# Two transformer layers on one core: ten weight loads issued with the MLP's groups instead of in a row

## The chip, the core and the metric

The kernel runs on one core of one Trainium2 chip. A core has five engines with queues of their own: TensorE (PE) multiplies matrices, VectorE (DVE) and ScalarE (ACT) work element by element, GpSimd (POOL) does small side work, and SyncE (SP) issues DMA transfers. ACT and POOL can issue transfers too. Each queue is worked off in order, and engines wait for each other by semaphores. The time is the device time of one execution in microseconds (us), the median of several runs.

## The reference

The input is 2048 rows of 512 numbers in bf16. The same two blocks, attention and MLP, are applied twice with the same weights. Each is added to its input, and each starts with a layer norm without gain or offset.

```python
def _A_ref(x, wqkv, wo):            # H = 32 heads of Dh = 16
    qkv = transpose((x @ wqkv).reshape(B, S, 3, H, Dh), 2, 0, 3, 1, 4)
    q, k, v = qkv[0], qkv[1], qkv[2]
    scores = jnp.einsum("bhqd,bhkd->bhqk", q, k) * (Dh ** -0.5)
    p = softmax(scores, axis=-1)
    o = jnp.einsum("bhqk,bhkd->bhqd", p, v)
    return transpose(o, 0, 2, 1, 3).reshape(B, S, D) @ wo

def _B_ref(x, w1, w2):              # w1 512 x 1792, w2 1792 x 512
    h = jnp.maximum(jnp.einsum("bsd,df->bsf", x, w1), 0)
    return jnp.einsum("bsf,fd->bsd", h, w2)

x = A_x
x = x + _A_ref(layernorm(x), A_wqkv, A_wo)
x = x + _B_ref(layernorm(x), B_w1, B_w2)
x = x + _A_ref(layernorm(x), A_wqkv, A_wo)
x = x + _B_ref(layernorm(x), B_w1, B_w2)
```

## The kernel before

**Chunks and segments.** The rows are cut into chunks `(l, j)`: four of 512 rows in the first layer (l = 0), and in the second (l = 1) two of 512 and four of 256, numbered j = 0 to 5. The attention of a chunk runs in segments, one for each half of a group of heads (T = 0 to 3, e = 0 or 1), so eight a chunk. In a segment the scores of blocks of 128 keys are made in `ps_s` (L1356), turned into exponentials `e` on ScalarE (L1365) or, for some blocks, by a chain of five steps on VectorE (`lin` L1051, `step` L1092, `cube` L1103 and L1107), and multiplied with the values into `ps_o` (L944).

**The end of a segment** (`finish_segment`, L828). VectorE copies `ps_o` into `u` (L858), among it the sums of the softmax. These few rows are brought into a compact shape by a small DMA on SyncE, `c<-u` (L863, 4 KB for 256 rows). VectorE takes the reciprocal (L885), and a second small DMA on SyncE brings it back, `u<-c` (L886). Then the reciprocals are spread over the lanes: for most segments by a DMA on GpSimd, `r<-u` (L888), for the last of a chunk by a shuffle on VectorE (L898). A multiplication (L874) gives `ot`. After the last segment of a chunk, the rest of that chunk's work is appended to a list.

**The rest of a chunk** (`rest_of_chunk`, L754): the product with `wo`, the norm, the first MLP product in groups (`h_group`, L687), the second (`z_group`), and in the first layer the next layer's keys and values. TensorE does these in pieces, between the scores of the chunks that follow.

**The weights of the first MLP product.** `w1` doesn't stay in the on-chip memory. Four buffers `w1buf` of 128 columns each are used in turn. A group of a 256-row chunk takes two of them, so there are seven groups; as soon as its last matmul has been written out, `after()` (L707) has SyncE load the two buffers again (`load_w1`, L677, its transfer at L681), which waits for TensorE to be done with them. The groups write through `ps_f` (L445), and VectorE applies the maximum with zero (`ht`, L701).

**The last 256 rows.** Their MLP is done at the end, in a part of its own, and finds all 14 blocks of `w1` in place: four in `w1buf`, ten in the buffers `kt01` and `kt2`, which held keys in the first layer and partial sums after that. The list `w1_last` names the 14 places (read at L1465). Where the ten are loaded is written in `rest_of_chunk`, when it is called for chunk (1, 3):

```python
if (l, j) == (1, LAST - 2):
    for ft in range(NF):
        home = (...)
        w1_last.append(home)
        if ft >= NW1:
            nc.sync.dma_start(out=home, in_=B_w1[:, ft * P : (ft + 1) * P]...)   # L766
```

**What sets the order.** The program keeps modelled clocks for TensorE, VectorE and ScalarE, and writes out instructions in the order these suggest. It allows a fixed time for each transfer: `C_LAG` 3600 ns from the copy to the reciprocal, `U_LAG` 3000 ns from the reciprocal to the shuffle, and 4000 ns for a load of `w1`. The load of the ten blocks takes no part in these clocks. The order on every engine is therefore fixed when the program is built, and SyncE's queue holds its transfers in the order in which they were written out.

Of the kernel before, what the change touches and what calls it, by code (L numbers as in the profile page):

```python
# [25 lines left out]
def kernel(  # L26
# [10 lines left out]
    nc = tc.nc  # L37
    P = 128
# [208 lines left out]
    def mark(key, engine="dve", lag=0.0):  # L247
        made[key] = (engine, (now_pe if engine == "pe" else now_dve)[0] + lag)

    def at(keys, engine):  # L250

        t = 0.0
        for k in keys:
            if k not in made:
                return None
            e, when = made[k]
            if e != engine:
                when += PE_TO_DVE if engine == "dve" else DVE_TO_PE
            elif e == "dve":
                when += DVE_TO_DVE  # L260
            t = max(t, when)
        return t
# [42 lines left out]
    def start_group(g):  # L305
        (urgent if g in urgent else work).remove(g)
        ready = max(at(g["deps"], "pe"), bank_free[0] + DVE_TO_PE)
        cur.extend((c, fn, ready if n == 0 else 0.0) for n, (c, fn) in enumerate(g["pieces"]))
# [28 lines left out]
    def do_task(t):  # L337
        dve_q.remove(t)
        dve_run(t["cost"], at(t["deps"], "dve"))
        t["fn"]()  # L340
        for k in t["makes"]:
            if k not in made:
                mark(k)
# [40 lines left out]
    def finish_group():  # L384
        while cur:
            do_piece()
        while evac:
            do_evac()
# [24 lines left out]
    def run_all():  # L413
        while True:
            finish_group()
            g = next(
                (g for q in (urgent, work) for g in q if at(g["deps"], "pe") is not None), None
            )
            if g is not None:
                start_group(g)  # L420
            elif dve_q:
                do_task(next(t for t in dve_q if at(t["deps"], "dve") is not None))
            else:
                break
        assert not (urgent or work)

    def mm_group(mms, fin, makes, deps, per=1, cost=EVAC, after=None, wide_by=QS, sums=1):


        hold = {}  # L430
        pieces = []
        n = len(mms)
        for a in range(0, n, per):

            def piece(a=a):
                if a == 0:
                    hold["b"] = bank()[:, 0 : sums * wide_by]
                b = hold["b"]
                for i in range(a, min(a + per, n)):
                    lhsT, rhs = mms[i]  # L440
                    k = n // sums
                    out = b[:, i // k * wide_by : (i // k + 1) * wide_by]
                    for g in range(4):
                        cols = slice(32 * g, 32 * g + 32)
                        nc.tensor.matmul(  # L445
                            out[cols], lhsT[:, cols], rhs, start=i % k == 0,
                            stop=i % k == k - 1, tile_position=(0, 32 * g),
                            skip_group_check=True,
                        )
                if a + per >= n:  # L450
                    put_evac(cost, lambda: fin(b))
                    if after:
                        after()

            pieces.append((min(per, n - a) * wide_by / QS, piece))
        return group(pieces, makes, deps)
# [8 lines left out]
    def columns(l, j):  # L465

        tt, n = chunks[l, j]
        return tt // TPC, tt % TPC * P, n * P
# [117 lines left out]
    def each(n, *key):  # L586
        return [key + (i,) for i in range(n)]
# [8 lines left out]
    def k_group(l, T, j):  # L596
        return mm_group(
            k_mms(T, j), lambda b: k_fin(l, T, j, b), [("k", l, T, j)],
            each(TPC, "xnT", ("ln1", l, j)),
        )  # L600
# [76 lines left out]
    def load_w1(n):  # L677

        if n < len(chunks) * NF - NF + NW1:
            ft = n % NF  # L680
            nc.sync.dma_start(  # L681
                out=w1buf[n % NW1][:],
                in_=B_w1[:, ft * P : (ft + 1) * P].rearrange("(c p) f -> p c f", p=P),
            )
            mark(("w1", n), "pe", 4000.0)

    def h_group(l, j, ft, war):  # L687
        n = (l * NQS + j) * NF + ft
        xj, a, w = columns(l, j)

        number = QS // w
        fts = range(ft, ft + number)
        made_here = [("h", l, j, f) for f in fts]

        def fin(b):
            out = htp[ft // 2][:, ft % 2 : ft % 2 + number, a : a + w]
            sums = b.rearrange("p (f q) -> p f q", f=number)
            if ending[0]:
                nc.scalar.activation(out=out, in_=sums, func=ACTF.Relu)
            else:  # L700
                nc.vector.tensor_scalar(  # L701
                    out=out, in0=sums, scalar1=0.0, scalar2=None, op0=ALU.max
                )
            for key in made_here:
                mark(key)

        def after():  # L707
            for f in range(number):
                load_w1(n + f + NW1)

        return mm_group(
            [
                (w1buf[(n + f) % NW1][:, c, :], xnT[xj][:, c, a : a + w])
                for f in range(number) for c in range(NDC)
            ],
            fin, made_here,
            each(w // P, "xnT", ("ln2", l, j)) + war + [("w1", n + f) for f in range(number)],
            after=after, wide_by=w, sums=number,
        )

# [19 lines left out]
    def before(l, j):  # L740

        if (l, j) == (0, 0):
            return None
        if not j:
            return 0, NQS - 1
        rows = chunks[l, j][0] % TPC
        return max(
            (l, b) for b in range(j)
            if chunks[l, b][1] == TPC or chunks[l, b][0] % TPC == rows
        )  # L750
# [3 lines left out]
    def rest_of_chunk(l, j):  # L754

        if (l, j) == (1, LAST - 2):
            for ft in range(NF):
                home = (
                    w1buf[((l * NQS + LAST) * NF + ft) % NW1] if ft < NW1
                    else (kt01 + kt2)[(ft - NW1) // 2][:, ft % 2, :].rearrange(  # L760
                        "p (c f) -> p c f", c=NDC
                    )
                )
                w1_last.append(home)
                if ft >= NW1:
                    nc.sync.dma_start(  # L766
                        out=home,
                        in_=B_w1[:, ft * P : (ft + 1) * P].rearrange("(c p) f -> p c f", p=P),
                    )
        b = before(l, j)  # L770
        xj, a, w = columns(l, j)
        n = w // P
        war_h = each(chunks[b][1], "z", *b) if b else []
        work[0:0] = [o_group(l, j, i) for i in range(n)] + ln_groups(
            ("ln2", l, j), xnT[xj], a, n, []
        )
        gs = [h_group(l, j, ft, war_h) for ft in range(0, NF, QS // w)]
        gs += [z_group(l, j, i) for i in range((l, j) == (1, LAST - 1), n)]
        if l == 0:
            gs += ln_groups(("ln1", 1, j), xnT[j], 0, TPC, [])  # L780
            gs.append(k_group(1, 0, j))
            gs += [v_group(1, kb) for kb in range(j * TPC, (j + 1) * TPC)]
            gs += [k_group(1, T, j) for T in range(1, 4)]
        return gs
# [344 lines left out]
    for e in range(2):  # L1129
        nc.vector.tensor_reduce(  # L1130
            out=mask[e],
            in_=ident[:].rearrange("p (g e d) -> p e g d", g=4, e=2)[:, e],
# [3 lines left out]
            out=qmask[:, e : e + 1], in0=mask[e], scalar1=SCALE * LOG2E * UNIT, scalar2=None,  # L1136
# [90 lines left out]
    while units:  # L1227
# [135 lines left out]
        while len(pend) == NE:  # L1363
            force_v()
        ex = nc.scalar.activation(  # L1365
            out=eb[:, 0 : place[m]], in_=b[:, 0 : place[m]], func=ACTF.Exp,
# [27 lines left out]
        run_dve(0.0, musts)  # L1394
    ending[0] = True
    run_all()
    ending[0], wide[0] = False, True
    users.clear()
    l, j = 1, LAST
# [11 lines left out]
    def at_bank(b):  # L1411
        n, w = b
        return ps_s[n][:, w, :] if n < 2 else (ps_f, ps_o)[n - 2][:]
# [46 lines left out]
    for ft in range(NF + 1):  # L1460
        if ft < NF:
# [6 lines left out]
            if ft % 2:  # L1468
                out = nc.scalar.activation(out=ht[ft][:, at_column : at_column + width], in_=at_bank(b)[:, 0:width], func=ACTF.Relu)
            else:  # L1470
                out = nc.vector.tensor_scalar(
                    out=ht[ft][:, at_column : at_column + width], in0=at_bank(b)[:, 0:width],
                    scalar1=0.0, scalar2=None, op0=ALU.max,
                )
# [7 lines left out]
    for i in rows:  # L1482
# [3 lines left out]
            out=out_flat[(tt + i) * P : (tt + i + 1) * P, :], in_=x_t[tt + i][:]  # L1486
# [31 lines left out]
```

The softmax here doesn't subtract the row's maximum and nothing guards it: scores larger than these inputs give would overflow.

## Time and profile before

| | |
|---|---|
| median of 4 runs | 1597.34 us (1596.12 to 1597.8) |
| profiled execution, its own time | 1597.56 us |
| its span, first to last instruction | 1595.7 us |
| ScalarE busy | 1554.3 us, 97% |
| VectorE busy | 1490.3 us, 93% |
| TensorE busy (matmuls) | 1441.6 us, 90% |
| mean granted TensorE clock | 0.993 |
| transfers at L681 (`w1`) | 130 of 128 KB |
| transfers at L766 (the ten blocks) | 10 of 128 KB, issued from 1373.5 to 1381.2 us |

Times in the views are us from the start of the span. In a list of waits, a row names the waiting engine, its line, what it waited for, the sum, the number of times and the longest. In a timeline, a row is start, duration, engine, line, operation, what is written from what, and how many instructions were merged; in brackets stands the idle time before it and what ended it. In a table of stretches, a row has its limits, its length, then for each engine the busy time and number of instructions (PE, weight loads, DVE, ACT, POOL), the granted TensorE clock, the share of the DMA engines and GB/s. SPq is SyncE's queue, in which a transfer's duration is that of its issue, not of the transfer.

### The profile page before, as it was taken

How to read it: one execution, taken by the hardware profiler on the slowest of the kernel's cores; microseconds unless marked ns; L12 is line 12 of the kernel's file. 1: busy time of each engine (PE TensorE's matmuls, PEld its weight loads, DVE VectorE, ACT ScalarE, POOL GpSimd, SP SyncE). 2: the span in 40 equal slices, each digit the busy share in tenths (PEclk: the TensorE clock that was granted, in tenths of full speed). 3: DMA queues.
4: the chain of work that ended last, by engine and by line, in shares of the span. 5: the costliest groups of instructions: out<-in, count | busy, mean ns of one | idle time of the engine just before them, and what ended most of it. 6: DMA issues, size and time to landing. Idle time of an engine off the chain costs nothing.

```text
span 1595.7 us, 45167 instructions
## 1 busy us (share of the span) xinstructions
PE 1441.6 (90%) x19793; PEld 538.0 (34%) x19793; DVE 1490.3 (93%) x2899; ACT 1554.3 (97%) x1383; POOL 98.3 (6%) x240
## 2 busy tenths in 40 slices
PE   8888888999999999899888999888999999899897
PEld 3322222322333222233222223222334444445444
DVE  6669999999999999999899999899999999899994
ACT  7999999999999999999999999999999999999994
POOL 2000001001010010100000000001000110010100
PEclk9999999999999999999999999999999999999999
DMA  5001100210012100120000100000211111413020
GB/s 166 2 1 23 20 11 11 46 29 11 7 22 44 20 15 5 30 46 10 14 2 11 31 8 1 2 4 8 55 24 20 33 36 26 93 20 65 14 61 16
DMA packets 115830, 42.42 MB, mean 27 GB/s; under 512 B 104785, under 2 KB 112721, under 8 KB 115633
## 3 DMA queue, kind: packets, MB, share of 16 engines
q1 hardware_dynamic: 101696, 26.21, 7.3%
q0 software_dynamic: 12592, 12.02, 4.2%
q8 instruction: 154, 2.52, 0.7%
q10 hardware_dynamic: 1344, 1.31, 0.2%
q14 instruction: 44, 0.35, 0.1%
HBM read 24.38 MB, written 2.10 MB: 17 GB/s over the span
## 4 chain that ended last, share of the span: by engine, by line
ACT 70%; PE 15%; DVE 11%; issue 2%; SPq 1%; DMA 0%; POOL 0%; ACTq 0%; DVEq 0%
ACT e L1365 70%; PE ps_s L1356 5%; PE ps_f L445 4%; PE ps_o L944 4%; DVE lin L1051 3%; DVE cube L1103 1%; DVE step L1092 1%; DVE cube L1107 1%; PE ps_s L1417 1%; DVE q L643 1%; DVE ht L701 1%; SPq L766 0%; DVE u L858 0%; DVE stats L479 0%; DVE x L727 0%
## 5 line engine op out<-in xcount | busy, mean ns | idle before, releaser
L1365 ACT ACTIVATE e<-ps_s 128x1536 bf16<-128x1536 f32 (+1 forms) x1366 | 1545.6, 1365 | 10.7 <-PE ps_s L1356 9.5
L1356 PE MATMUL ps_s<-q,ktp 32*128 32x512 bf16 (+1 forms) x6121 | 607.5, 342 | 104.7 <-ACT e L1365 94.8
L944 PE MATMUL ps_o<-e,vaug 128*32 128x512 bf16 (+1 forms) x4256 | 497.5, 346 | 12.0 <-DVE u L858 4.9
L1051 DVE TENSOR_SCALAR lin<-ps_s 128x512 int16<-128x512 f32 x684 | 465.4, 685 | 26.8 <-PE ps_s L1356 20.0
L1356 PEld LDWEIGHTS <-ktp 32*128 32x128 bf16 x6121 | 195.5, 92 | 553.1 <-issue 418.9
L944 PEld LDWEIGHTS <-vaug 128*32 128x32 bf16 x6036 | 171.9, 94 | 300.1 <-issue 283.5
L1092 DVE TENSOR_SCALAR step<-lin 128x1024 int16<-128x1024 int16 x684 | 268.9, 419 | 0.6
L1103 DVE TENSOR_TENSOR cube<-step 128x1024 f16<-128x1024 bf16 x342 | 231.8, 681 | 0.6
L1107 DVE TENSOR_TENSOR cube<-cube,lin 128x1024 bf16<-128x1024 f16 x342 | 232.2, 680 | 0.0
L944 PE MATMUL ps_o<-step,vaug 128*32 128x512 bf16 (+1 forms) x864 | 156.2, 340 | 2.7 <-DVE step L1092 2.7
L445 PE MATMUL ps_f<-xnT,w 128*32 128x512 bf16 (+1 forms) x2016 | 150.3, 346 | 6.2 <-DVE ht L701 2.8
L944 PE MATMUL ps_o<-cube,vthird 128*32 128x512 bf16 (+1 forms) x812 | 148.8, 338 | 0.5 <-DVE cube L1107 0.5
L445 PE MATMUL ps_f<-w,ht 128*32 128x512 bf16 x1624 | 146.8, 381 | 1.1 <-DVE q L643 0.8
L944 PE MATMUL ps_o<-lin,vaug 128*32 128x512 bf16 (+1 forms) x864 | 122.4, 340 | 4.8 <-DVE u L858 1.8
L888 POOL DMA_DIRECT2D r<-u x59 | 43.5, 737 | 1179.4 <-DVE lin L1051 426.5
L445 PE MATMUL ps_f<-xnT,wqkv 128*32 128x512 bf16 (+1 forms) x1312 | 107.2, 362 | 5.6 <-DVE ktp L593 0.9
L445 PE MATMUL ps_f<-wo,ot 128*32 128x512 bf16 x960 | 86.3, 381 | 1.1 <-DVE ktp L593 0.8
L701 DVE TENSOR_SCALAR ht<-ps_f 128x512 bf16<-128x512 f32 x105 | 72.0, 685 | 2.5 <-PE ps_f L445 1.2
L445 PEld LDWEIGHTS <-w 128*32 128x32 bf16 x2016 | 59.5, 96 | 37.4 <-issue 21.7
L643 DVE TENSOR_TENSOR q<-ps_f,masks 128x1024 bf16<-128x1024 f32 (+1 forms) x51 | 53.6, 1051 | 12.4 <-PE ps_f L445 7.7
L944 PEld LDWEIGHTS <-vthird 128*32 128x32 bf16 x812 | 44.6, 95 | 30.8 <-issue 27.1
L445 PEld LDWEIGHTS <-ht 128*32 128x32 bf16 x1624 | 45.3, 96 | 28.3 <-issue 12.2
(103 smaller groups left out, 637.6 us busy)
## 6 DMA issues: line engine op xcount, KB each, us to landing
w<-in_B_w_dram SPq DMA_DIRECT2D x130, 128.0 KB
r<-u POOLq DMA_DIRECT2D x32, 256.0 KB, 7.4
r<-u POOLq DMA_DIRECT2D x27, 128.0 KB, 4.9
out_dram<-x SPq DMA_DIRECT2D x16, 128.0 KB
x<-in_A_x_dram SPq DMA_DIRECT2D x14, 128.0 KB
w<-in_B_w_dram SPq DMA_DIRECT2D x1, 1792.0 KB
ktp<-in_B_w_dram SPq DMA_DIRECT2D x10, 128.0 KB
wqkv<-in_A_wqkv_dram ACTq DMA_DIRECT2D x2, 512.0 KB
```

What stands on the lines that cost most here:

```text
L445: nc.tensor.matmul(out[cols], lhsT[:, cols], rhs, start=i % k == 0, stop=i % k == k - 1, tile_position=(0, 32 * g), skip_group_check=True,)
L643: return nc.vector.tensor_mul(out=qbuf[n % 2][:, :, 0:w], in0=b.rearrange("p (e q) -> p e q", e=1).to_broadcast((P, 2, w)), in1=qmask.rear ...
L701: nc.vector.tensor_scalar(out=out, in0=sums, scalar1=0.0, scalar2=None, op0=ALU.max)
L888: nc.gpsimd.dma_start(out=r[:, 0:width], in_=bass.AP(tensor=sums.tensor, offset=sums.offset, ap=[list(sums.ap[0]), [0, 32], [1, width]],),)
L944: nc.tensor.matmul(ps_o[32 * g : 32 * g + 32, 0 : sg["w"]], values[:, 4 * sg["T"] + g, 2 * e : 2 * e + 32], rhs, start=g not in sg["begun" ...
L1051: first = nc.vector.tensor_scalar(out=lin[which][:, half * QS : (half + 1) * QS], in0=src, scalar1=EXP_BIAS, scalar2=0.0, op0=ALU.add, op1 ...
L1092: nc.vector.tensor_scalar(out=stair, in0=line, scalar1=keep, scalar2=put, op0=ALU.bitwise_and, op1=ALU.bitwise_or,)
L1103: (609, lambda: nc.vector.tensor_mul(out=power, in0=mantissa, in1=mantissa)),
L1107: (609, lambda: nc.vector.tensor_mul(out=power.bitcast(BF16), in0=power, in1=line.bitcast(BF16))),
L1356: nc.tensor.matmul(b[:, a : a + sg["w"]], kt[32 * g : 32 * g + 32, kc : kc + P], qbuf[sg["n"] % 2][32 * g : 32 * g + 32, sg["e"], 0 : sg[" ...
L1365: ex = nc.scalar.activation(out=eb[:, 0 : place[m]], in_=b[:, 0 : place[m]], func=ACTF.Exp, scale=1.0 / (LOG2E * UNIT),)
L1417: uses(nc.tensor.matmul(out, lhsT, rhs, start=first, stop=last), b, needs=needs)
```

## The change

The ten transfers are no longer issued in `rest_of_chunk`. It puts their places and block numbers into a list `w1_to_load` instead. Each time that `after()` of a group of the first MLP product is run, it issues the loads of that group's own buffers as before, and then takes one entry from the list, if there is one, and issues its load. At the end of the attention, an assertion says that the list is empty. The transfers themselves, their number and their places are the same.

```diff
+    w1_to_load = deque()
+
     def h_group(l, j, ft, war):
...
         def after():
             for f in range(number):
                 load_w1(n + f + NW1)
+            if w1_to_load:
+                home, of = w1_to_load.popleft()
+                nc.sync.dma_start(
+                    out=home,
+                    in_=B_w1[:, of * P : (of + 1) * P].rearrange("(c p) f -> p c f", p=P),
+                )
...
                 w1_last.append(home)
                 if ft >= NW1:
-                    nc.sync.dma_start(
-                        out=home,
-                        in_=B_w1[:, ft * P : (ft + 1) * P].rearrange("(c p) f -> p c f", p=P),
-                    )
+                    w1_to_load.append((home, ft))
...
     run_all()
+    assert not w1_to_load
```

## The prediction

> **What bounds the kernel.** The page comes first: ScalarE is busy for 97% of the span, nearly all of it the exponentials at L1365, and the busy slices show it full in the middle of the run. Whatever shortens the run must take out a gap between two exponentials. So the next view is the list of waits, cut to the stretch in which the ten loads are issued (1360 to 1470 us):
>
> ```profile
> ACT e L1365 <- PE ps_s L1356: 3.4, 2, 2.8
> DVE c L885 <- DMA c<-u: 3.3, 1, 3.3
> PE ps_o L944 <- DVE step L1092: 2.7, 1, 2.7
> ```
>
> Three engines stop once each for about 3 us, in a stretch where the exponentials otherwise lose nothing. The timelines of SyncE's queue, VectorE and ScalarE give the order:
>
> ```profile
> 1372.93 0.54 SPq L886 DMA_DIRECT2D u<-c  x1
> 1373.52 8.20 SPq L766 DMA_DIRECT2D ktp<-in_B_w_dram  x10
> 1381.81 0.56 SPq L863 DMA_DIRECT2D c<-u  x1
> 1382.48 2.29 SPq L681 DMA_DIRECT2D w<-in_B_w_dram  x4
> 1384.95 0.55 SPq L886 DMA_DIRECT2D u<-c  x1
> 1386.40 6.14 SPq L681 DMA_DIRECT2D w<-in_B_w_dram  x4
> ...
> 1376.40 0.41 DVE L858 COPY u<-ps_o 128x256 f32<-128x256 f32 x1
> ...
> 1383.79 0.20 DVE L885 RECIPROCAL c<-c 128x8 f32<-128x8 f32 x1 [3.31 <-DMA c<-u]
> ...
> 1387.34 0.44 DVE L898 STREAM_SHUFFLE r<-u 128x256 f32<-128x256 f32 x1
> ...
> 1386.85 1.45 ACT L1365 ACTIVATE e<-ps_s 128x1536 bf16<-128x1536 f32 x1 [2.82 <-PE ps_s L1356]
> 1388.87 3.52 ACT L1365 ACTIVATE e<-ps_s 128x1024 bf16<-128x1024 f32 x3 [0.57 <-PE ps_s L1356]
> ```
>
> The ten loads hold the queue for 8.2 us. Right behind them stands the 4 KB transfer c<-u (L863), which carries the softmax sums of the segment that has just ended. Its data are there at 1376.8 (the copy at 1376.40), but it starts at 1381.81, and VectorE, which works in order, stands at the reciprocal until 1383.79. TensorE then lacks step (L1092), and ScalarE lacks scores. The chain of waits runs through this place too: it names L766 ten times, then "DMA c<-u" for 1.95 us, then the reciprocal. One more view, the stretches of 3.41 us around it, with one from elsewhere that ends in the same way:
>
> ```profile
> 1380.11:1383.53 3.42, 2.70 (x71) 1.64 (x64) 0.37 (x1) 3.42 (x4) 0.00 (x0) 1.00 0.64 139
> 1383.53:1386.94 3.41, 1.40 (x39) 0.98 (x42) 3.15 (x8) 0.59 (x2) 0.00 (x0) 1.00 0.71 157
> 1386.94:1390.35 3.41, 3.41 (x60) 2.10 (x52) 3.01 (x8) 2.84 (x3) 0.00 (x0) 0.50 0.37 82
> 383.42:386.83 3.41, 2.16 (x22) 0.70 (x21) 3.41 (x8) 3.41 (x5) 2.88 (x6) 1.00 0.01 2
> ```
>
> The number after POOL's is the granted TensorE clock: after the stretch in which TensorE was busy for only 1.40 us it falls to 0.50 for 3.41 us.
>
> **What the gap costs.** Exponentials overlap a little, so I take start to start: undisturbed, 0.90 us for 1024 columns and 1.33 us for 1536 (medians of the trace). Around the gap: 1382.89 to 1386.85 is 3.97 us for a 1024, a loss of 3.06; 1386.85 to 1388.87 is 2.02 for a 1536, a loss of 0.69; 1389.79 to 1390.94 is 1.15 for a 1024, a loss of 0.24. Sum 3.99 us: the first term is the wait, the other two lie in the half-clock stretch. From there to 1560 us ScalarE stays full, so everything later moves up by what is won here.
>
> **The change, part by part.**
>
> *Removed: ten loads in a row.* c<-u then starts when the copy is done. Elsewhere the copy takes about 0.44 us from its start to the start of c<-u (copy at 1393.12, c<-u at 1393.56), so it starts at 1376.85 and with 1.95 us lands at 1378.8. VectorE reaches the reciprocal at 1380.40 (the op ahead starts at 1379.80 and holds the engine for 0.60). Slack 1.6 us: this wait goes.
>
> *Added: one load behind each group's own two w1 loads.* Which groups? The list is filled where the ten were issued. In the queue before, eight w1 loads stand behind the ten and ahead of 1393 us: four groups of two, still of the third chunk of layer two. So four loads go with them, and six with the fourth chunk's groups (1436 to 1459 us), not with the fourth and fifth. Call the four groups A to D. One load takes SyncE about 0.51 us to issue (five of the ten; 1.2 to 1.6 us when the queue is backed up).
>
> *What they push back.* The new order is c<-u, A's two loads and one more, B's two and one more, u<-c, then C and D. A w1 load waits for TensorE to be done with the buffer it overwrites: B's second load can go at 1381.2 us, when B's matmuls end. It takes 0.4, the added load 0.5, the queue's own waits 0.1: u<-c starts at 1382.27 and, at 2.0 us like c<-u, lands at 1384.27. Who waits for it is the shuffle at L898. Before, it came 3.55 us after the reciprocal; now 1380.40 + 3.55 = 1383.95, and some later, as two operations ahead of it need TensorE's results first (ht needs B's, about 0.15 us; lin needs the scores issued at 1382.19, about 0.15). So it is due near 1384.25, just as its data land. Bounds: nothing, to 0.75 us with u<-c 0.5 us late and the shuffle 0.25 early; I take nothing to 0.1, because u<-c took 2.0 us at 1384.95 with four w1 loads just ahead.
>
> *C and D.* Their reloads come behind 0.5 us more each, D's end near 1393.1 on the old clock against the next c<-u at 1393.56. No cost; without that half microsecond, c<-u would slip into a lag of some 4 us.
>
> *Fourth chunk.* The tightest place is c<-u at 1440.08, directly behind four w1 loads: two added loads put it to about 1440.6. Its reciprocal ran at 1445.13, 2.8 us after the landing of about 1442.3: covered. The last loads are issued by 1457 us; their first use is in the last rows' MLP, after 1577 us. Cost nothing. Bytes, matmuls, activations and the order on the other engines stay.
>
> *The clock.* [...] By the rows, half clock follows stretches that are merely thin: 1.40 us busy here, 2.16 at 383 us, while 2.70 left the clock alone. I take the rows: with the gap filled TensorE is busy for about 2.9 to 3.4 us of each stretch, and the drop goes.
>
> [...]
>
> *Sum.* 3.99, less about 0.15: TensorE resumes at 1382.63 instead of 1385.54, so the first scores are ready at about 1383.94, while ScalarE is free at 1383.80. 3.84, less up to 0.1 for the shuffle: 3.75 us. The profiled execution took 1597.56 us (span 1595.7), 0.2 us above the median, so 1593.8 there and **1593.6** against the median of 1597.34, 0.23% faster. A measurement of this kernel can tell about 0.2%, 3.2 us, from no change; the forecast is only just past it.
>
> **The rivals.**
>
> *The wait moves to u<-c.* u<-c now stands behind six weight loads, which an r<-u transfer (128 KB, 4.9 us median) shares the engines with until about 1380.5. If it lands 0.8 to 1.5 us late, the shuffle holds VectorE, which had nearly no slack in the old gap (3.31 us of wait became 3.06 of loss): gain 2.3 to 3.0, 1594.3 to 1595.1. For it: the planner allows 3 us from reciprocal to shuffle, and 2.0 of these are the transfer. Against: the 2.0 us at 1384.95 under a similar queue.
>
> [...]
>
> *The change does nothing it should:* something else stops VectorE at the same place, as the w1 reloads of A, which also came late before. They are issued at 1377.8 and 1378.5 now, and group C needs them at 1382.6; little room for this. About 1597.
>
> *Slower: TensorE waits for w1 in the fourth chunk.* The r<-u at 1435.6 makes w1 loads slow: the first was issued at 1436.02, landed about 1440.9, and is used at 1441.45, with 0.6 us to spare. Added loads share these engines. If each of the six takes the 1.6 us of the longest issue, pushed on from group to group, TensorE loses 6 x 1.6 - 0.6 = 9.0 us, net 5.2: 1602.5. It decides from about 1.2 us a load on. Against it: the added load stands behind its own group's reloads, and later groups have 2 us and more.
>
> **How the numbers follow.** Forecast 0.77, the wait at u<-c 0.11, the clock 0.04, nothing 0.03, slower 0.05. The forecast's own range is 1592.8 to 1594.4 (the bounds above and the spread of the medians, 1596.12 to 1597.8). The range reaches over the first two rivals and leaves out the last two: 1592.6 to 1595.8. Faster by over 0.2% means under 1594.15: most of the forecast, 0.69, and 0.01 of the rest; the u<-c and clock cases, the forecast's slow end and "nothing" are within 0.2%: 0.25; slower 0.05.
>
> **What would show it.** c<-u issued within 0.5 us of its copy near 1376.9; no DMA wait at L885; exponentials without a gap at 1383 to 1391; clock 1.00 there; four added loads ahead of 1393 us and six at 1433 to 1455. Wrong it would be if a wait stands at L898, at the matmuls that read w1, or if a half-clock stretch appears somewhere new.

## The result and the profile after

The changed kernel takes 1593.75 us (median of 35 runs, 1590.57 to 1599.33) against 1597.67 (56 runs) of the kernel before, so these medians differ by 3.92 us. The ratio on record is 0.9973, 95% interval 0.9966 to 0.9979, which would be 4.3 us less with an interval of 3.4 to 5.4. The forecast was 3.75 us less. Single executions spread over 9 to 11 us, more than the change is worth, so below one figure is used that is read inside a profile: **the interval** from the start of the `c<-u` of the segment before the chunk's last one to the first addition of the product with `wo` (`x<-x,ps_f`, L667). It holds the place of the change and leaves out what happens elsewhere. In the kernel before it runs from 1365.83 to 1397.46 us, 31.63; in the changed one from 1364.75 to 1392.64, 27.89. The difference is 3.74 us.

The changed kernel's timelines of SyncE's queue, VectorE and ScalarE at the same place (the added loads are now at L714, and later lines have moved by 2 to 8):

```profile
1371.85 0.54 SPq L891 DMA_DIRECT2D u<-c  x1
1375.77 0.56 SPq L868 DMA_DIRECT2D c<-u  x1
1376.44 1.74 SPq L681 DMA_DIRECT2D w<-in_B_w_dram  x2
1378.23 0.50 SPq L714 DMA_DIRECT2D ktp<-in_B_w_dram  x1
1379.70 1.05 SPq L681 DMA_DIRECT2D w<-in_B_w_dram  x2
1380.80 0.50 SPq L714 DMA_DIRECT2D ktp<-in_B_w_dram  x1
1381.46 0.54 SPq L891 DMA_DIRECT2D u<-c  x1
...
1375.33 0.41 DVE L863 COPY u<-ps_o 128x256 f32<-128x256 f32 x1
...
1379.33 0.19 DVE L890 RECIPROCAL c<-c 128x8 f32<-128x8 f32 x1
...
1383.65 0.43 DVE L903 STREAM_SHUFFLE r<-u 128x256 f32<-128x256 f32 x1
...
1373.68 26.52 ACT L1370 ACTIVATE e<-ps_s 128x1536 bf16<-128x1536 f32 x23
```

`c<-u` starts 0.44 us after the start of its copy, the reciprocal has no wait in its row, and 23 exponentials run without a gap. The list of waits of this kernel (1360 to 1470 us) has no wait at the reciprocal left, but a small new one:

```profile
PE ps_s L1361 <- ACT e L1370: 4.2, 13, 0.5
...
DVE r L903 <- DMA u<-c: 0.4, 1, 0.4
```

TensorE still waits for ScalarE, but no exponential waits for TensorE any more. In the table of stretches the half-clock stretch is gone:

```profile
1380.00:1383.41 3.41, 3.41 (x93) 2.21 (x90) 3.12 (x7) 3.41 (x4) 0.00 (x0) 1.00 0.65 141
1383.41:1386.82 3.41, 2.98 (x77) 1.82 (x74) 3.17 (x8) 3.41 (x4) 0.00 (x0) 1.00 0.52 117
```

Between the two profiled executions the time fell by 3.12 us (1597.56 to 1594.44), less than the 3.74. The changed kernel's profile is already 1.08 us ahead at 1365 us, far from the change, and it loses 1.68 us at the very end (29.42 us from the start of the last exponential to the end of the span, instead of 27.74). That part is taken up last.

### The profile page after: what moved, and what is told of

It reads as the page before. It is cut to its first block, busy times and chain, and to the rows that moved or that the text cites. A ratio compares the mean times of both kernels' runs of the same rounds, so it can differ in the third digit from the quotient of the medians.

```text
span 1592.5 us, 45173 instructions
## 1 busy us (share of the span) xinstructions
PE 1438.9 (90%) x19793; PEld 537.9 (34%) x19793; DVE 1490.2 (94%) x2899; ACT 1553.4 (98%) x1383; POOL 98.0 (6%) x240
## 4 chain that ended last, share of the span: by engine, by line
ACT 72%; PE 14%; DVE 11%; issue 2%; DMA 1%; POOL 0%; ACTq 0%; DVEq 0%
ACT e L1370 72%; PE ps_s L1361 5%; PE ps_f L445 4%; PE ps_o L949 4%; DVE lin L1056 3%; DVE cube L1108 1%; DVE step L1097 1%; DVE cube L1112 1%; PE ps_s L1423 1%; DMA wqkv<-in_A_wqkv_dram 1%; DVE ht L703 1%; DVE q L643 0%; DVE u L863 0%; DVE x L735 0%; DVE ktp L593 0%
## 5 line engine op out<-in xcount | busy, mean ns | idle before, releaser
L949 PEld LDWEIGHTS <-vthird 128*32 128x32 bf16 x812 | 44.3, 95 | 30.7 <-issue 27.1
```

The costliest lines, as they stand in the source:

```text
L949: nc.tensor.matmul(ps_o[32 * g : 32 * g + 32, 0 : sg["w"]], values[:, 4 * sg["T"] + g, 2 * e : 2 * e + 32], rhs, start=g not in sg["begun" ...
```

## The experiments

The theory, from the prediction: what counts is **where `c<-u` and `u<-c` stand in SyncE's queue**. The rival: **the burst**, ten loads together crowding the DMA engines, slows whatever transfer is near. All edits are against the changed kernel, unless it is said otherwise. The numbers of all runs stand in a table behind the last of them.

### The row, but behind `u<-c`

The loads are taken out of `after()` and issued in `recip()`:

```diff
             nc.sync.dma_start(out=sums, in_=c)
+            while w1_to_load:
+                home, of = w1_to_load.popleft()
+                nc.sync.dma_start(out=home, in_=B_w1[...])
```

> All ten in a row, but directly behind the u<-c of the segment that ends the chunk, and no load with the groups. The queue's order: neither c<-u nor u<-c stands behind a load of the ten; no wait at the reciprocal, at the shuffle less than the changed kernel's 0.40 us; the ten hold the queue for about 8 us, to about 1389.5 on the clock of the changed kernel, so the next c<-u starts about 2 us late and still lands before its reciprocal at 1394.8. Interval 27.5 to 27.9, the whole 1593.5 us as the changed kernel. The burst: about 3 us are lost to waits for transfers near it, interval about 31, the whole about 1597 us.

Measured: interval 27.67, time 1593.7 us (ratio 0.9960, 0.9945 to 0.9975). SyncE's queue in this kernel:

```profile
1374.49 0.56 SPq L862 DMA_DIRECT2D c<-u  x1
1375.16 4.18 SPq L681 DMA_DIRECT2D w<-in_B_w_dram  x4
1379.45 0.54 SPq L885 DMA_DIRECT2D u<-c  x1
1380.03 6.75 SPq L888 DMA_DIRECT2D ktp<-in_B_w_dram  x10
1386.89 2.09 SPq L681 DMA_DIRECT2D w<-in_B_w_dram  x4
1389.07 0.56 SPq L862 DMA_DIRECT2D c<-u  x1
```

Ten loads in a row hold the queue for 6.75 us and cost nothing, since neither small transfer of this segment stands behind them; VectorE, ScalarE and TensorE wait for no DMA in the stretch. The next `c<-u` does stand behind them: it starts 1.8 us late, lands in 2.40 us, and is there 1.8 us before its reciprocal. So being in a row didn't cost anything by itself here, and the 31 of the burst theory did not come: `u<-c`, just ahead of the ten, landed in 1.98 us. What a row does to a small transfer close behind it is not tested by this.

### The row between `c<-u` and `u<-c`

```diff
-            if w1_to_load:
+            while w1_to_load:
                 home, of = w1_to_load.popleft()
```

> All ten in a row with the first group behind the chunk's end, so behind c<-u and ahead of u<-c. The queue's order: no wait at the reciprocal, but u<-c starts some 5 to 6 us later than in the changed kernel (ten loads of 0.5 us, some held up to 1.6), and the shuffle waits 5 to 6 us; interval 32 to 33.5, the whole 1597.5 to 1599 us, so no better than before or worse. If only c<-u mattered, the interval would be 27.9 and the whole 1593.7 us. The burst: about 31.

Measured: interval 33.97, half a microsecond over the range expected, and time 1600.18 us (ratio 1.0010, 1.0001 to 1.0020). The row takes 6.83 us to issue, and the wait is at the shuffle now (list of waits of VectorE and ScalarE, 1366 to 1400 us):

```profile
DVE r L903 <- DMA u<-c: 5.4, 1, 5.4
...
ACT e L1370 <- PE ps_s L1361: 5.8, 2, 4.8
```

The same ten loads at the first group behind the chunk are worse than in the old place. TensorE's weight loads wait 3.2 us for `w1` here too, but end before the maximum `ht` behind the shuffle, for which the matmuls wait 4.4 us. Getting `c<-u` out from behind them is not enough; `u<-c` must be out as well.

### Seven, nine and five in the old place

```diff
                 if ft >= NW1:
-                    w1_to_load.append((home, ft))
+                    if ft - NW1 < 7:
+                        nc.sync.dma_start(out=home, in_=B_w1[...])
+                    else:
+                        w1_to_load.append((home, ft))
```

> Seven of the ten loads stay in a row in the old place, the other three go one by one with the groups behind it. The theory of the queue's order: the seven hold SyncE's queue until about 1378.0 us (the seventh load of before ended there), c<-u then lands at about 1380.0, just ahead of the reciprocal's turn at 1380.4. So no wait or under 0.3 us there, and nearly the whole gain: from the start of the c<-u of the segment before to the first row's addition of the product with wo, 31.63 us in the kernel before and 27.89 in the changed one, it should show 27.8 to 28.3; the whole about 1593.8 us. The theory of the burst (the ten in a row crowd the DMA engines and slow whatever is near): seven tenths of the wait stay, about 2.3 us, interval 30.5.

> Nine of the ten in a row, one behind. The queue's order: the nine hold the queue until 1381.2 us, c<-u lands at about 1383.2, wait at the reciprocal about 2.7 us, interval (as for the row of seven) 30.7 to 31.3, the whole about 1597 us. Two loads more than seven so cost nearly all of the gain. The burst: nine tenths of the wait, 3.0 us, interval 31.2; the two theories differ at seven, not here. Clock: if a gap on TensorE of about 2 us already makes a half-clock stretch, one stands behind it; if it takes the whole 2.7 us of before, none.

With nine, the reciprocal waited 3.2 us (2.7 expected), the interval was 30.55 (30.7 to 31.3 expected) and the time 1598.23 us (ratio 1.0000, 0.9987 to 1.0013). With seven the expectation failed: a wait of 2.3 us and an interval of 30.21, which is what the burst theory had said (1596.65 us, ratio 0.9986, 0.9974 to 0.9998). SyncE's queue with seven:

```profile
1371.24 0.54 SPq L897 DMA_DIRECT2D u<-c  x1
1371.83 7.14 SPq L775 DMA_DIRECT2D ktp<-in_B_w_dram  x7
1379.07 0.56 SPq L874 DMA_DIRECT2D c<-u  x1
1379.74 0.97 SPq L681 DMA_DIRECT2D w<-in_B_w_dram  x2
```

Seven loads hold the queue for 7.14 us, nearly as long as ten (8.20). One by one: 0.47, 1.24, 0.51, 0.51, 0.51, 2.30 and 1.36 us. `c<-u` itself lands 1.96 us after its start, as in the kernel before (1.95). So the delay is in the issue, and 0.51 us or less holds for four of these seven loads alone; the first five take 3.24 us together. A row of five should then be free:

> Five of the ten in a row in the old place, five one by one behind. The rows of seven and nine showed that the loads don't take 0.55 us each: the first five to six go at that pace, then the seventh and eighth are held 1.2 to 2.3 us each. The queue's order with this held-up queue: five loads end about when the copy is done, c<-u starts within 0.3 us of its earliest place, no wait at the reciprocal; u<-c as in the changed kernel, with a wait at the shuffle of 0.2 to 0.6 us; interval 27.6 to 28.1, the whole about 1593.7 us. The burst: half of the wait stays, 1.6 us, interval about 29.7.

Measured: `c<-u` starts 0.24 us after its earliest place and the reciprocal doesn't wait. But the shuffle waits 1.1 us, interval 28.59, time 1594.47 us (ratio 0.9983, 0.9976 to 0.9991). The hold-up has gone to the next loads in the queue: the two of the first group took 1.59 and 1.27 us to issue, and `u<-c` stands behind them. Its half on `c<-u` held, its interval did not.

### What holds the queue

This edit is against the kernel before:

```diff
+                part = 8 if (l, j, t) == (1, LAST - 2, NT - 2) else width
                 nc.gpsimd.dma_start(
-                    out=r[:, 0:width],
+                    out=r[:, 0:part],
```

(with `part` for `width` in the source too.)

> The kernel before, all ten in a row in the old place; only the r<-u of the segment ahead of the chunk's last one copies 8 of its 256 columns, so that the spread reciprocals of these other columns are left out and stay those of an earlier segment. It asks why the queue is held for 8.2 us and not for ten times 0.55. If r<-u, in flight at the same time on the same DMA engines, holds the loads: none takes over 0.7 us to issue, the ten hold the queue for about 5.5 us, c<-u starts near 1379.1 on the clock of the kernel before and lands at 1381.1, wait at the reciprocal about 0.7 us, interval about 28.4. If the ten fill the queue by themselves: the hold stays near 8 us, wait 3 us, interval 31.6.

SyncE's queue of this kernel, and the wait at the reciprocal:

```profile
1372.70 0.54 SPq L886 DMA_DIRECT2D u<-c  x1
1373.29 5.93 SPq L766 DMA_DIRECT2D ktp<-in_B_w_dram  x10
1379.32 0.56 SPq L863 DMA_DIRECT2D c<-u  x1
```

```profile
DVE c L885 <- DMA c<-u: 2.0, 1, 2.0
```

With a small `r<-u` nine of the ten issue in 0.51 us each (the first took 0.98), 5.93 us in all: 2.3 of the 8.2 us were due to GpSimd's transfer. It is not the only thing that holds a load: in the row behind `u<-c` no `r<-u` is in flight, and one of the ten still took 1.49 us; what held that one stays open. The interval is 29.26, not 28.4, because `c<-u` took 2.90 us to land instead of 1.95, with ten loads close ahead of it. So the burst theory has a part after all: close behind a row that took 5.93 us to issue, the transfer itself was late by about 1 us (by 0.6 us in the row of five, which has the whole `r<-u` in flight as well). This kernel ran once (1596.62 us), which says nothing of its time.

### The row on GpSimd's queue

```diff
-                    w1_to_load.append((home, ft))
+                    nc.gpsimd.dma_start(out=home, in_=B_w1[...])
```

> All ten in a row in the old place of the program, but issued by GpSimd, none with the groups. The bytes and the burst stay, SyncE's queue is free. The queue's order: c<-u starts 0.45 us after its copy, no wait or under 0.5 us at the reciprocal; interval 27.6 to 28.6, the whole 1593.3 to 1594.5 us. The burst: c<-u and u<-c or the w1 loads of the groups arrive late by some 3 us together, interval about 31, the whole about 1597 us.

`c<-u` started on time and landed in 2.43 us, 1.3 us before the reciprocal. But `u<-c`, issued at 1380.49 us, took 5.63 us to land, and the four w1 loads ahead of it 5.2 to 6.4 (2.5 to 2.7 for the four w1 loads ahead of `u<-c` in the kernel before). The list of waits, 1362 to 1400 us:

```profile
DVE r L909 <- DMA u<-c: 2.9, 1, 2.9
ACT e L1376 <- PE ps_s L1367: 2.3, 2, 1.2
...
PE ps_f L445 <- DMA w<-in_B_w_dram: 0.9, 1, 0.9
```

Interval 30.63, time 1595.95 us (ratio 0.9987, 0.9980 to 0.9995). Here the burst theory was right: the queue of the small transfers was free, and the transfers were late. While `u<-c` is under way, the share of the DMA engines (the last figure but one) is 1.14 here, and 0.76 in the changed kernel (second line):

```profile
1380.49:1386.12 5.63, 4.39 (x106) 2.49 (x97) 2.73 (x6) 4.61 (x5) 2.17 (x3) 1.00 1.14 213
1381.46:1383.61 2.15, 2.15 (x64) 1.50 (x64) 1.73 (x4) 2.15 (x3) 0.00 (x0) 1.00 0.76 165
```

### What the new wait costs, and whether it can go

Two loads with each group, and none until `u<-c` has been issued (a flag set in `recip()`):

```diff
-            if w1_to_load:
+            for _ in range(min(2, len(w1_to_load))):
```

```diff
-            if w1_to_load:
+            if w1_to_load and sums_back[0]:
```

> Two of the ten with each group, so done after five groups. u<-c of the chunk's last segment then stands behind two more loads, about 1.0 us later, and the shuffle waits about 1.4 us where the changed kernel has 0.40. This measures what such a wait costs: with no slack the interval grows from 27.89 to 28.9, with the 0.25 us of slack that the old wait had (3.31 us waited, 3.06 lost) to about 28.6; if the shuffle is off the path that ScalarE waits for, it stays at 27.9. The whole 1593.7 to 1594.9 us.

> As the changed kernel, but no load is taken from the list until the u<-c of the chunk's last segment has been issued: the first two groups go without, so two loads go with the third chunk's last groups, seven with the fourth's and one with the fifth's. The shuffle's wait of 0.40 us should be gone, the interval 27.5 to 27.9. If the wait cost something, the whole is up to 0.4 us under the changed kernel, 1593.3; if it lay in slack, equal. No measurable difference is expected.

> The changed kernel itself, beside the others of this call on the same chip. Every theory: interval 27.9, wait at the shuffle 0.4 us, the whole 3.5 to 4.3 us under the kernel before. A second profile shows whether the clock stays at 1.00 at the place of the old gap.

Two each: the shuffle waits 1.5 us and the interval is 28.99. None before `u<-c`: no wait, 27.67. The changed kernel once more: 0.2 us of wait, 27.68, and a clock of 1.00 from 402 to 1566 us. The times are 1593.79, 1593.44 and 1593.64 us (ratios 0.9974, 0.9969 and 0.9965, each about 0.0012 either way), which can't be told apart. Waits at the shuffle of 0.2, 0.4, 1.1 (the row of five) and 1.5 us make the interval 0.01, 0.22, 0.92 and 1.32 longer than 27.67. So about 0.2 us of such a wait were free here, and what was over that was paid in full. No version was measurably faster than the changed kernel.

| loads (all times in us) | wait at reciprocal | wait at shuffle | interval |
|---|---|---|---|
| ten in a row, old place (before) | 3.3 | 0 | 31.63 |
| seven in a row, old place | 2.3 | 0.7 | 30.21 |
| nine in a row, old place | 3.2 | 0 | 30.55 |
| five in a row, old place | 0 | 1.1 | 28.59 |
| ten, old place, small `r<-u` | 2.0 | 0 | 29.26 |
| ten, old place, GpSimd's queue | 0 | 2.9 | 30.63 |
| ten in a row at the first group | 0 | 5.4 | 33.97 |
| ten in a row behind `u<-c` | 0 | 0 | 27.67 |
| two with each group | 0 | 1.5 | 28.99 |
| one each, from `u<-c` on | 0 | 0 | 27.67 |
| one with each group (changed) | 0 | 0.4 | 27.89 |
| the same again | 0 | 0.2 | 27.68 |

Taken over 27.67, the interval is longer by the sum of the two waits less 0.2 to 0.5 us in seven of the ten rows with a wait. In the kernel before (3.96 us) and with the row at the first group (6.30) it is longer by more than the waits; these two have half-clock stretches in the interval (1386.94 to 1390.35 and 1388.36 to 1395.18 us). With the row on GpSimd's queue (2.96) it is longer by just the wait; there TensorE waits for w1 as well. The times of the whole runs agree: the change of each interval from 31.63 lies in the 95% interval that was measured for that kernel's time, but for the row behind `u<-c` (3.96 us, against 4.0 to 8.8).

## Why the prediction was right

**The wait at the reciprocal goes.** Right in place and size: `c<-u` starts 0.44 us after its copy, as worked out, and lands in 1.85 us (1.95 taken).

**Which groups carry the loads.** Right: four added loads ahead of 1393 us, six from 1432.6 to 1450.8 us.

**`u<-c` arrives just as the shuffle is due.** It was worked out to start 1.87 us after the start of the reciprocal, and starts 2.13 after it. It lands in 2.15 us (2.0 taken), and the shuffle waits 0.40 us, within the bounds of 0 to 0.75. The cost, taken as 0 to 0.1, is 0.22 (27.89 less 27.67) in this profile and 0.01 in the second one.

**No cost later.** Right in its result: the next `c<-u` starts 0.45 us after its copy, and in the fourth chunk there is no wait at a reciprocal, a shuffle or w1. But the price of 0.51 us for an added load was too low: with an `r<-u` in flight two took 1.75 and 2.19 us to issue, and two without one 0.91 and 0.85. The slack covered it: `c<-u` still lands 1.8 us or more before its reciprocal there.

**The sum.** 3.75 forecast, 3.74 measured in the interval. That it fits to the last digit is luck: two small misses cancel. The 0.15 us taken off because the first scores would come a little late was not lost: the two kernels with no wait left are 3.96 us under the kernel before, nearly all of the 3.99 that were counted for the gap; and the shuffle cost 0.22 instead of up to 0.1.

**The clock term was right for these two profiles and not as sure as it was put.** The prediction counted 0.93 us for the half-clock stretch and said that merely thin stretches bring it about, which the profiles show only in part. The row of nine has nearly the same gap on TensorE and no half-clock stretch behind it (the kernel before first, then nine):

```profile
1385.54 0.29 PE L944 MATMUL ps_o<-step,vaug 128*32 128x256 bf16 x2 [2.73 <-DVE step L1092]
1387.97 0.29 PE L955 MATMUL ps_o<-step,vaug 128*32 128x256 bf16 x2 [2.66 <-DVE step L1103]
```

The row of seven has a stretch thinner than the 2.16 us that was quoted (1.74), and keeps its clock too. In the profile of the kernel before, the times from one change of the clock to the next are 6.83, 184.32, 3.41, 474.45, 6.83, 324.27, 3.41 and 204.80 us, which is 2, 54, 1, 139, 2, 95, 1 and 60 times 3.413; in the changed kernel's they are 10.24, 1167.36, 3.41 and 23.89 us, 3, 342, 1 and 7 times as much. Points this far apart, counted on from a change in the same profile, are called edges here. In the next two tables the stretches lie between such edges. First nine:

```profile
1383.23:1386.64 3.41, 2.08 (x49) 1.02 (x40) 0.42 (x2) 3.31 (x3) 0.00 (x0) 1.00 0.64 139
1386.64:1390.06 3.42, 2.09 (x60) 1.45 (x60) 3.39 (x9) 0.78 (x1) 0.00 (x0) 1.00 0.73 163
1390.06:1393.47 3.41, 3.07 (x77) 1.87 (x74) 3.41 (x8) 3.41 (x4) 0.00 (x0) 1.00 0.35 79
```

Then seven:

```profile
1380.02:1383.44 3.42, 1.74 (x50) 1.12 (x41) 2.39 (x6) 2.33 (x3) 0.00 (x0) 1.00 0.85 189
1383.44:1386.85 3.41, 3.05 (x75) 1.67 (x68) 2.72 (x7) 2.74 (x3) 0.00 (x0) 1.00 0.53 114
```

With nine an edge cuts the gap in half, 1.3 us on each side, 2.08 and 2.09 us busy, and the clock stays at 1.00; in the kernel before 2.0 of the 2.73 us lay in one stretch, with 1.40 busy. The interval with nine is 1.08 us shorter, though its wait is shorter by only 0.1. So the 0.93 us seem to belong to the profiled execution. That an execution with other edges would have lost about 3.06 is the author's estimate, 3.99 less 0.93; no second profile of the kernel before shows it. The length of the gap doesn't sort the cases: one of 2.73 us had a half-clock stretch behind it there, one of 2.66 us had none here, and the fall at the end of the changed kernel's run, shown below, follows a stretch whose longest gap is 0.54 us. The prediction's reading, that thin stretches come ahead of it, holds only one way. Ahead of 1590 us the clock falls to 0.50 four times in the profile of the kernel before, each time behind a stretch, between edges, with 1.40 to 2.27 us busy, and twice in that of the changed kernel, behind 1.86 and 2.46 us. But stretches as thin keep the clock: one with 2.22 us at 1100 us in the changed kernel, and the one with 1.74 in the row of seven. What decides between them is open.

**The rivals.** The wait at `u<-c` is real, but 0.40 us instead of 0.8 to 1.5; the runs with two each and with all at the first group show where it would have decided. Longer waits of TensorE for w1 (over 0.2 us) appeared only with the row on GpSimd's queue and with the row at the first group. For the case in which the half clock stays (0.04 of the forecast's chances) no run shows a ground: with the gap filled, the clock was 1.00 in this place in both profiles of the changed kernel.

## What to carry to other kernels

A large load that nobody needs soon can stop an engine all the same, by standing ahead of a small transfer that is needed soon (3.3 us at the reciprocal here). Look at what follows it in its queue, and where that transfer's answer goes back through the same queue, clear the way back too. Don't take the issue time of one load times their number: here seven loads held the queue nearly as long as ten (7.14 and 8.20 us), and ten took 5.93 us when another queue's transfer was made small. And moving the loads to another queue helped little here (1.0 of the 4.0 us in the interval): the share of the DMA engines was 1.14 instead of 0.76, and `u<-c` and the w1 loads landed late (5.63 us instead of about 2.0 for `u<-c`).

## What was not expected

**The end of the run.** The changed kernel's profile loses 1.68 us behind the last exponential, to a half-clock stretch that the profile of the kernel before doesn't have. The stretches of the changed kernel and of the row behind `u<-c` there, again between edges:

```profile
1560.99:1564.41 3.42, 2.46 (x31) 1.30 (x27) 0.04 (x2) 2.91 (x3) 0.00 (x0) 1.00 0.00 0
1564.41:1567.82 3.41, 3.41 (x9) 1.22 (x8) 2.92 (x5) 0.00 (x0) 0.00 (x0) 0.50 0.02 5
```

```profile
1560.72:1564.13 3.41, 2.76 (x24) 1.45 (x24) 1.00 (x3) 1.90 (x3) 0.00 (x0) 1.00 0.02 5
1564.13:1567.55 3.42, 3.42 (x18) 1.53 (x17) 2.03 (x5) 0.69 (x2) 0.00 (x0) 1.00 0.00 0
```

The work is the same; where the edges lie in it is not. In the two profiles of the changed kernel, which both have this stretch, the last exponential starts 2.0 and 2.1 us behind an edge; in those of the kernel before, of the row behind `u<-c` and of the row of nine, which don't have it, 0.1, 1.0 and 1.9 us. That this decides is the author's guess, which no run tested. The ten-in-a-row kernel with the small `r<-u` has it too (29.29 us to the end), so the spread loads aren't needed to bring it. Whether it comes equally often with the kernel before and the changed one was not counted: of these there are one profile without it and two with it. The ratios of the row behind `u<-c`, whose profile hasn't got it, and of the changed kernel measured again can't be told apart, 0.9960 and 0.9965.
